# Layer 1's gate weights in two loads instead of four, and pair 0's scores moved ahead of pair 15's maximum product in layer 2

## The chip, the cores and the metric

The kernel runs on one core of a Trainium2 chip. The metric is the time of one execution on the device in microseconds (us); lower is better. Most executions of one kernel agree within 0.3%. The profile of a kernel is one execution taken by the hardware profiler; its span is some 1.4 us shorter than the time of the same execution.

## The reference

The program is a decode step of two identical layers for one token of width 640, in bf16: attention over the last 4096 cached positions, with 32 heads of 192, then a gated MLP of width 1536. Weights are the same in both layers, and so are the caches.

```
x = x + attention(layernorm(x))      # q = x@wq; scores with 4096 keys; softmax; values; @wo
x = x + mlp(layernorm(x))            # (sigmoid(x@w_gate) * (x@w_up)) @ w_down
# and both once more
```

There is one token, so every weight and every cached value is used for one matrix-vector product. The work is reading: 218.7 MB.

## The kernel before

Heads are taken in 16 pairs. A pair has an "a" part (query weights and keys) and a "b" part (values and output weights), 3.6 MB each, in one of seven slots of on-chip memory. MLP weights pass through a smaller region of cells; one cell holds one of the 12 blocks of 128 MLP columns. Layer 2 begins with pairs 14, 15, 0 and 1, most of which are still in memory from layer 1.

All loads stand in one list, `seq`, and are issued in that order from one queue, by SyncE (SP). A load waits until its destination has been read for the last time. So a late product on TensorE (PE) makes the next load late. That matters only if the queue has nothing else left to do by then.

The gate weights (`wg`) and what reuses their cells (cut):

```python
    MW = {"wg0": (0, 0, 3), "wg1": (3, 3, 6), "wg2": (6, 6, 9), "wg3": (9, 9, 12), "u0": (12, 0, 2), "u1": (14, 2, 7),
          "d0": (0, 0, 3), "d1": (3, 3, 6), "u2": (6, 7, 10), "u3": (9, 10, 12), "d2": (11, 6, 9), "d3": (14, 9, 12)}
    #     name: (first cell, first block, end block)
    MAFTER = {"d0": ("wg0",), "d1": ("wg1",), "u2": ("wg2",), "u3": ("wg3",), "d2": ("wg3", "u0"), "d3": ("u1",)}
    ...
            c, f0, f1 = MW[k]
            src = {"w": wg_d, "u": wu_d, "d": wd_d}[k[0]]
            pg.dma(q_dma(mreg(c * FW, (f1 - f0) * FW), src[:, f0 * FW:f1 * FW]), k, wr=rc[c:c + f1 - f0])
```

The first down load `d0` goes into the cells of `wg0`, the third up load `u2` into those of `wg2`. The product is in four parts of three blocks, in the same order.

The start of layer 2's attention (cut). `QK` is the 24 score matmuls of a pair, `soft` takes the maximum on VectorE (DVE) and spreads it over the partitions by the "maximum product" on PE, and `expo` is the exponent on ScalarE (ACT):

```python
            soft(0, scale_pm)                    # pair 14
            expo()
            ET(0)
            Q(0, 0)
            soft(1, hook=lambda: Q(2, None))     # pair 15: max, then the hook, then the maximum product
            for i in (2, 0, 1):
                ...                              # three copies on DVE
            expo(1)                              # pair 15
            QK(0, 0)                             # pair 0's scores; frees slot 4
            soft(0, mid=lambda: PVmm(14, 0))     # pair 0's maximum
```

## Time and profile before

| | |
|---|---|
| time, median of 3 runs | 514.11 us (513.99 to 514.98) |
| span of the profiled run | 512.7 us |
| bytes read, mean rate | 218.7 MB, 427 GB/s |
| busy: 16 DMA engines / PE / DVE / ACT | 99% / 51% / 20% / 17% |

From the profile page of the kernel before: span, busy time of the engines, busy tenths of the DMA engines in 40 slices, packets, the queue that carries the loads (packets, MB, share of 16 engines' span), and the chain of work that ended last by engine.

```profile
span 512.7 us, 8580 instructions
PE 260.9 (51%) x3716; PEld 136.9 (27%) x3716; DVE 100.4 (20%) x379; ACT 84.8 (17%) x171; POOL 4.2 (1%) x31
DMA  9999999999999999999999999999999999999996
DMA packets 9820, 218.71 MB, mean 427 GB/s; under 512 B 1224, under 2 KB 1608, under 8 KB 4808
q1 hardware_dynamic: 9656, 218.37, 99.2%
DMA 63%; PE 23%; DVE 7%; ACT 3%; issue 2%; SPq 2%; DVEq 0%; POOL 0%; ACTq 0%; POOLq 0%
```

The queue table decides: the 16 DMA engines are busy from end to end. The last line alone could mislead. The chain of waits runs through PE for 23% of the span, because a load's issue waits for a product; but while it waits, the queue is still working on older loads.

The useful number is therefore the **backlog**: the landing of the load before, less the issue of this one. It is how long the queue still has to work when a load is added. A load is split over 16 engines, which signal one by one; "landing" here is the last of the 16. From the trace of the kernel before:

| load (bytes per row) | issued | landed | backlog at issue |
|---|---|---|---|
| last gate load (3840) | 261.41 | 277.48 | 14.9 |
| second up load, u1 (6400) | 264.00 | 280.18 | 14.3 |
| first down load, d0 (3840) | 275.25 | 281.34 | 4.9 |
| third up load, u2 (3840) | 276.97 | 283.71 | 5.5 |
| refill of pair 0's slot (28416) | 304.09 | 319.75 | 7.3 |
| first load of the late loop (56832) | 363.72 | 387.39 | 6.9 |

After the first loads it is never below 4.5 us.

The stretch where the gates are used, from the timeline of the kernel before (start us, length us, engine, line, operation, output and inputs, count, and in brackets the idle time before it and what ended that). The gate product is four times 15 matmuls, the first two merged:

```profile
274.69 1.11 PE L675 MATMUL scores<-sh,big 128*128 128x1 bf16 x30 [0.35 <-DVE sc L371]
275.25 0.90 SPq L214 DMA_DIRECT2D big<-in_wd_dram  x2
276.38 0.56 PE L675 MATMUL scores<-sh,big 128*128 128x1 bf16 x15 [0.58 <-DMA big<-in_wg_dram]
276.97 1.48 SPq L214 DMA_DIRECT2D big<-in_wu_dram  x2
277.53 0.56 PE L675 MATMUL scores<-sh,big 128*128 128x1 bf16 x15 [0.59 <-DMA big<-in_wg_dram]
```

The first two parts wait for the layernorm, not for weights. The third and fourth wait for their loads, and each releases a load 0.6 us later.

The start of layer 2, from the same view: pair 15's own scores, pair 15's maximum (DVE L439), its maximum product (PE L445), pair 0's scores (PE L429), the three copies (DVE L170), the refill that the scores release, and pair 0's maximum.

```profile
293.51 1.48 PE L429 MATMUL o<-big,qs 128*32 128x512 bf16 x24
298.80 1.22 DVE L439 TENSOR_REDUCE sc<-o 128x1 f32<-128x1024 f32 x1
300.57 0.79 PE L445 MATMUL bank<-diag,sc 128*128 128x128 f32 x2 [1.02 <-ACT diag L442]
301.29 2.75 PE L429 MATMUL scores<-big,qs 128*32 128x512 bf16 x24
301.83 1.94 DVE L170 TENSOR_SCALAR big<-bank 128x507 uint32<-128x507 uint32 x3
304.09 0.33 SPq L214 DMA_DIRECT2D big<-in_uc_dram  x1
304.10 1.23 DVE L439 TENSOR_REDUCE sc<-scores 128x1 f32<-128x1024 f32 x1 [0.32 <-PE scores L429]
```

PE is idle for 1.02 us before the maximum product, although pair 0's scores could run there.

### The profile page before, as it was taken

How to read it: one execution, taken by the hardware profiler on the slowest of the kernel's cores; microseconds unless marked ns; L12 is line 12 of the kernel's file. 1: busy time of each engine (PE TensorE's matmuls, PEld its weight loads, DVE VectorE, ACT ScalarE, POOL GpSimd, SP SyncE). 2: the span in 40 equal slices, each digit the busy share in tenths (PEclk: the TensorE clock that was granted, in tenths of full speed). 3: DMA queues.
4: the chain of work that ended last, by engine and by line, in shares of the span. 5: the costliest groups of instructions: out<-in, count | busy, mean ns of one | idle time of the engine just before them, and what ended most of it. 6: DMA issues, size and time to landing. Idle time of an engine off the chain costs nothing.

```text
span 512.7 us, 8580 instructions
## 1 busy us (share of the span) xinstructions
PE 260.9 (51%) x3716; PEld 136.9 (27%) x3716; DVE 100.4 (20%) x379; ACT 84.8 (17%) x171; POOL 4.2 (1%) x31
## 2 busy tenths in 40 slices
PE   0452456344634454326566767873625244634665
PEld 0221222122312221112234434432312122312334
DVE  0221221111210221112121243321202111210311
ACT  1110111011101111011121033130301011101220
POOL 0010000000000000000000000000000000000000
PEclk9995555566556566675575578665857556556675
DMA  9999999999999999999999999999999999999996
GB/s 426 430 423 426 427 430 428 426 435 448 439 430 426 440 430 430 426 435 457 399 422 416 418 440 436 435 430 427 443 443 443 430 426 426 440 431 417 431 427 275
DMA packets 9820, 218.71 MB, mean 427 GB/s; under 512 B 1224, under 2 KB 1608, under 8 KB 4808
## 3 DMA queue, kind: packets, MB, share of 16 engines
q1 hardware_dynamic: 9656, 218.37, 99.2%
q8 instruction: 13, 0.21, 0.1%
q10 hardware_dynamic: 144, 0.06, 0.0%
q14 instruction: 7, 0.06, 0.0%
HBM read 218.43 MB, written 0.00 MB: 426 GB/s over the span
## 4 chain that ended last, share of the span: by engine, by line
DMA 63%; PE 23%; DVE 7%; ACT 3%; issue 2%; SPq 2%; DVEq 0%; POOL 0%; ACTq 0%; POOLq 0%
DMA big<-in_uc_dram 54%; PE scores L429 9%; PE o L488 7%; DMA big<-in_wd_dram 6%; DMA big<-in_wu_dram 3%; DVE sc L439 3%; PE bank L445 2%; PE bank L411 2%; SPq L214 2%; ACT e_sb L453 2%; PE bank L523 1%; PE bank L459 1%; ACT diag L442 1%; DVE sc L471 1%; PE o L469 1%
## 5 line engine op out<-in xcount | busy, mean ns | idle before, releaser
L429 PE MATMUL scores<-big,qs 128*32 128x512 bf16 x744 | 83.6, 619 | 10.3 <-DVE qs L417 9.6
L411 PE MATMUL bank<-sh,big 128*128 128x1 bf16 x465 | 17.2, 166 | 133.3 <-DMA big<-in_uc_dram 130.9
L488 PE MATMUL o<-big,et_sb 128*2 128x384 bf16 x1024 | 76.1, 465 | 6.1 <-DMA big<-in_uc_dram 3.6
L442 ACT ACTIVATE diag<-cst,sc 128x128 f32<-128x128 bf16 x32 | 12.8, 401 | 310.2 <-DVE sc L439 299.3
L439 DVE TENSOR_REDUCE sc<-scores 128x1 f32<-128x1024 f32 x31 | 37.9, 1224 | 79.1 <-PE scores L429 79.1
L411 PEld LDWEIGHTS bank<-sh,big 128*128 128x128 bf16 x465 | 14.7, 104 | 136.5 <-DMA big<-in_uc_dram 113.2
L445 PE MATMUL bank<-diag,sc 128*128 128x128 f32 x64 | 21.8, 436 | 46.7 <-ACT diag L442 46.7
L453 ACT ACTIVATE e_sb<-scores,sc 128x1024 bf16<-128x1024 f32 x31 | 37.3, 1204 | 39.7 <-DVE sc L448 37.4
L417 DVE TENSOR_TENSOR qs<-bank,cst 128x96 bf16<-128x96 f32 x30 | 7.7, 258 | 163.6 <-PE bank L411 163.6
L488 PEld LDWEIGHTS o<-big,et_sb 128*2 128x2 bf16 x1024 | 27.8, 106 | 41.7 <-issue 28.6
L429 PEld LDWEIGHTS scores<-big,qs 128*32 128x32 bf16 x744 | 24.2, 134 | 45.0 <-issue 33.2
L495 ACT CAST o_sb<-o 128x384 bf16<-128x384 f32 x64 | 29.6, 474 | 21.4 <-PE o L488 21.3
L445 PEld LDWEIGHTS bank<-diag,sc 128*128 128x128 f32 x64 | 13.6, 265 | 71.5 <-ACT diag L442 70.5
L523 PE MATMUL bank<-sh,big 128*128 128x1 bf16 x480 | 17.3, 165 | 15.5 <-DVE sh L512 14.9
L463 DVE CAST et_sb<-bank 128x64 bf16<-128x64 f32 x32 | 7.2, 225 | 69.8 <-PE bank L459 69.8
L523 PEld LDWEIGHTS bank<-sh,big 128*128 128x128 bf16 x480 | 14.6, 99 | 18.0 <-DVE sh L512 12.4
L446 DVE TENSOR_REDUCE sc<-bank 128x2 f32<-128x128 f32 x32 | 9.3, 292 | 40.1 <-PE bank L445 40.1
L459 PE MATMUL bank<-cst,e_sb 128*128 128x8 bf16 x256 | 11.7, 169 | 7.8 <-ACT e_sb L453 7.6
L459 PEld LDWEIGHTS bank<-cst,e_sb 128*128 128x128 bf16 x256 | 9.0, 101 | 23.9 <-issue 17.4
L469 PE MATMUL o<-sc 128*128 128x2 f32 x62 | 13.8, 292 | 0.6 <-ACT o_sb L495 0.6
L469 PEld LDWEIGHTS o<-sc 128*128 128x128 f32 x62 | 11.9, 239 | 1.9 <-ACT o_sb L495 1.3
L471 DVE RECIPROCAL sc<-o 64x1 f32<-64x1 f32 x62 | 10.2, 164 | 10.0 <-PE o L469 8.2
(78 smaller groups left out, 105.9 us busy)
## 6 DMA issues: line engine op xcount, KB each, us to landing
big<-in_uc_dram SPq DMA_DIRECT2D x20, 7104.0 KB, 22.7
big<-in_uc_dram SPq DMA_DIRECT2D x11, 3552.0 KB, 21.4
big<-in_uc_dram SPq DMA_DIRECT2D x2, 3072.0 KB, 18.8
big<-in_uc_dram SPq DMA_DIRECT2D x7, 480.0 KB, 6.5
big<-in_uc_dram SPq DMA_DIRECT2D x1, 2784.0 KB, 12.3
big<-in_uc_dram SPq DMA_DIRECT2D x1, 2304.0 KB, 10.0
big<-in_uc_dram SPq DMA_DIRECT2D x1, 2048.0 KB, 11.7
big<-in_wg_dram SPq DMA_DIRECT2D x4, 480.0 KB, 15.1
```

The source lines that it names most:

```text
L411: ins = t.matmul(qe[:, i:i + 1], lhsT=w[:, c * 2 * DH + c0:c * 2 * DH + c0 + P], rhs=xq[:, c:c + 1], start=(c == 0), stop=(c == DC - 1))
L429: ins = t.matmul(sc_x[1 + b][32 * j:32 * j + 32, :], lhsT=qs[:, y, k, :], rhs=slot(sa, WQE + k * W + (4 * b + j) * 512, 512), start=(k == ...
L439: pg.op("dve", lambda v: v.reduce_max(out=mx, in_=sc_x[0][:], axis=AX.X), wr=[res("mx")], ex=sc_x[3:5])
L442: pg.op("act", lambda a: a.mul(out=diag[:], in_=ident, mul=mx), rd=[res("cst"), res("mx")], wr=[res("diag")])
L445: pg.op("pe", lambda t: t.matmul(dmx[:, 0:P], lhsT=ones_f, rhs=diag[:], start=True, stop=True), rd=[res("diag"), res("ones")], ex=[rb[2]])
L453: pg.op("act", lambda a: a.activation(out=e_sb[:], in_=sc_x[0][:], func=ACT.Exp, bias=nbias, scale=srs_c, accum_out=rowsum), rd=[res("nbia ...
L459: ins = t.matmul(qe[:, 0:2 * NB].rearrange("p (r x) -> p r x", r=2)[:, :, 4 * b:4 * b + 4], lhsT=e_sb[:, b * P:(b + 1) * P], rhs=sel, star ...
L469: pg.op("pe", lambda t: t.matmul(sm, lhsT=ones_f, rhs=rs2[z], start=True, stop=True), rd=[res(f"rs2{z}"), res("ones")], wr=[res("rsum")], ...
L471: rb[bk].last["dve"] = pg.op("dve", lambda v, h=h: v.reciprocal(out=Rn[z][64 * h:64 * h + 64], in_=sm[64 * h:64 * h + 64, h:h + 1]), rd=[r ...
L488: ins = t.matmul(o8[h][32 * j:32 * j + 2, 0:2 * DH].rearrange("p (a d) -> p a d", a=2), lhsT=et_sb[:, z, h * NB + 2 * u:h * NB + 2 * u + 2 ...
L495: pg.op("act", lambda a, h=h: a.copy(out=o8_sb[:, :, h * DH:(h + 1) * DH], in_=o8[h][:, 0:2 * DH].rearrange("p (a d) -> p a d", a=2)), wr= ...
L523: ins = t.matmul(yT[:, j:j + 1], lhsT=wo[:, c * D + j * P:c * D + (j + 1) * P], rhs=oTb[z][:, c:c + 1], start=False, stop=(c == 2), skip_g ...
```

## The change

The intent: larger and fewer transfers for the gate weights, and PE's gap in layer 2 filled, with a slot freed earlier.

```diff
+    MD = {"wg0": (0, 0, 6), "wg2": (6, 6, 12), **{k: v for k, v in MW.items() if k[0] != "w"}}
...
-    ... [(k,) for k in (*MW, "v1", ...)] ...
+    ... [(k,) for k in (*MD, "v1", ...)] ...
...
-            c, f0, f1 = MW[k]
+            c, f0, f1 = MD[k]
...
-            soft(1, hook=lambda: Q(2, None))
+            soft(1, hook=lambda: (Q(2, None), QK(0, 0)))
...
             expo(1)
-            QK(0, 0)
             soft(0, mid=lambda: PVmm(14, 0))
```

The product is still in four parts, but the first two now wait for one load and the last two for the other. One line was added, so line numbers after it are one higher.

More of the change, by code (lines that the diff above doesn't have):

```diff
@@ L229, in decode_kernel @@
     seq = [("a", 0, 0)] + [("c", 0, p) for p in range(1, 15)] + [("a", 0, 15), ("b", 0, 14)] + last_values(0, 15)
-    seq += [("wol", 14), ("wol", 15)] + [(k,) for k in (*MW, "v1", "wq2", "v0", "v2", "v3", "v4", "wq3", "wom")] + [("a0", 1), ("a0", 2), ("a", 1, 3), ("b", 1, 2)]
+    seq += [("wol", 14), ("wol", 15)] + [(k,) for k in (*MD, "v1", "wq2", "v0", "v2", "v3", "v4", "wq3", "wom")] + [("a0", 1), ("a0", 2), ("a", 1, 3), ("b", 1, 2)]
     seq += [("b", 1, 3), ("a", 1, 4), ("b", 1, 4), ("a", 1, 5), ("a", 1, 6), ("b", 1, 5)]
@@ L299, in try_load @@
             pg.dma(q_dma(slot(s, o, WOE), b_in(it[1], o, o + WOE)), f"wol{it[1]}", wr=[res(f"wol{it[1]}")], extra=ev_done["b1" if it[1] == 15 else "b14"])
-        elif k in MW:
+        elif k in MD:
             if any("done_" + n not in ev_done for n in MAFTER.get(k, ())):
                 return False
-            c, f0, f1 = MW[k]
+            c, f0, f1 = MD[k]
             src = {"w": wg_d, "u": wu_d, "d": wd_d}[k[0]]
```

## The prediction

> **What bounds the kernel.** The 16 DMA engines. The queue table puts queue 1 at 99.2% of 16 engines' span; 218.7 MB in 512.7 us is 427 GB/s. PE is busy 51%, DVE 20%, ACT 17%. Pairing each issue in the trace with its landing gives the backlog, the time the queue still had to work when the next load was issued: never below 4.5 us after the start. Tightest are layer 1's MLP (issues at 275 to 290 us: 4.5 to 5.7 us) and the steady loops (5.2 to 7). The first load's first packet began 1.0 us after its issue, the last store's 1.3 us after, so 4.5 us is enough. A compute change counts only if it lets the backlog run out, or changes what the engines carry.
>
> **Gate weights in two loads.** Four 480 KB loads (rows of 3840 B) become two of 960 KB (rows of 7680 B). In the trace a 3840 B packet takes 149 ns and a 7680 B one 291 ns: 7 ns saved for each of 256 packets, over 16 engines 0.11 us; two loads' completion writes (9 ns each on every engine) add 0.02 us. Two issues of 0.43 us go from SP, but SP was 13 to 15 us ahead there, so that is worth nothing. The direction agrees with the Trainium skill, "Perfetto Trace Analysis", section "DMA Optimizations" (larger transfers use bandwidth better), but here it is 2% on under 1% of the bytes.
>
> The cost: the first six blocks land together near 275.1 us, so the gate product starts there, not at 274.66; the second six near 277.4, where its first half had been there at 276.33. Loads that reuse the cells go later: first down load 275.25 to about 275.8, third up load 276.97 to about 278.05. Backlog falls by about 1 us at most, to some 4.3 us, still enough: no time lost.
>
> **Pair 0's scores earlier.** PE runs the 24 score matmuls (2.75 us) at about 299.5 us, in the 1.0 us gap before pair 15's maximum product (300.57), not after it. Pair 0's slot is released about 1.7 us earlier: its refill is issued at about 302.4 instead of 304.09. But the maximum product moves to about 302.3, pair 15's exponent from 301.93 to about 303.6, and three copies on DVE that stand before pair 0's maximum from 301.83 to about 303.5; pair 0's maximum goes from 304.10 to about 305.4. The compute chain gets 1 to 1.4 us longer until about 345 us. Backlog at those issues is 7 to 18 us, so neither gain nor loss reaches the end; from 363 us the loop is paced by landings again.
>
> **Sum.** About -0.13 us on the DMA stream, 0 from the rest: 514.0 us, range 513.3 to 514.7, wide because the runs before span 513.99 to 514.98. Faster by over 2%: 0.005; within 2%: 0.99; slower: 0.005.
>
> **What would show it.** Right: queue 1 still about 99% and 427 GB/s; 256 packets of 7680 B for 512 of 3840 B; last gate load landing within 0.2 us of 277.4; maximum product about 1.7 us later and pair 0's maximum later, while loads from 350 us land within 0.3 us of before. Wrong: a gap in DMA near 278 to 284 us, or landings from 290 us on shifted by over 0.5 us.
>
> **What would make it wrong.** If a load under traffic needs much more than 1.3 us from issue to data, the smaller backlog in the MLP starves the engines and costs up to 1 us; or the packet rate drifts between builds by more than the effect, a quarter of a thousandth.

## The result, and the profile after

| | median | runs |
|---|---|---|
| before | 514.05 us | 6, 513.75 to 514.98 |
| changed | 514.02 us | 6, 513.67 to 514.52 |
| ratio | 0.9998 | 95% interval 0.9985 to 1.001 |

A ratio is the mean time of one kernel's fast runs over that of the other's fast runs of the same rounds, so it is not quite the ratio of the medians. The result is "the same".

The same lines of the page for the changed kernel:

```profile
span 513.1 us, 8577 instructions
PE 265.5 (52%) x3716; PEld 140.1 (27%) x3716; DVE 100.4 (20%) x379; ACT 84.8 (17%) x171; POOL 4.3 (1%) x31
DMA  9999999999999999999999999999999999999996
DMA packets 9532, 218.71 MB, mean 426 GB/s; under 512 B 1192, under 2 KB 1576, under 8 KB 4520
q1 hardware_dynamic: 9368, 218.37, 99.2%
DMA 64%; PE 23%; DVE 7%; ACT 2%; issue 2%; SPq 1%; DVEq 0%; ACTq 0%
```

Bytes are the same, and q1 has 288 packets fewer: 256 of data and 32 that signal the completion of two loads. Its share stays at 99.2%.

The loads, from the list of DMA issues on the pages (count, KB each, median us from issue to landing), before and then after:

```profile
big<-in_wg_dram SPq DMA_DIRECT2D x4, 480.0 KB, 15.1
```

```profile
big<-in_wg_dram SPq DMA_DIRECT2D x2, 960.0 KB, 16.1
```

The gate stretch of the changed kernel, from its timeline:

```profile
274.98 0.96 PE L675 MATMUL scores<-sh,big 128*128 128x1 bf16 x30 [0.88 <-DMA big<-in_wg_dram]
275.56 0.80 SPq L215 DMA_DIRECT2D big<-in_wd_dram  x2
277.27 0.96 PE L675 MATMUL scores<-sh,big 128*128 128x1 bf16 x30 [1.34 <-DMA big<-in_wg_dram]
277.87 0.80 SPq L215 DMA_DIRECT2D big<-in_wu_dram  x2
```

Both halves of the product now wait for their load. The first down load goes out 0.3 us later than before, and the third up load 0.9 us later. Their backlogs are 4.3 and 4.6 us.

The start of layer 2 of the changed kernel, from the same view:

```profile
293.72 2.75 PE L430 MATMUL o<-big,qs 128*32 128x512 bf16 x24
300.59 1.22 DVE L440 TENSOR_REDUCE sc<-o 128x1 f32<-128x1024 f32 x1
301.29 2.75 PE L430 MATMUL scores<-big,qs 128*32 128x512 bf16 x24
303.97 0.49 PE L446 MATMUL bank<-diag,sc 128*128 128x128 f32 x2
304.09 0.33 SPq L215 DMA_DIRECT2D big<-in_uc_dram  x1
304.94 1.94 DVE L170 TENSOR_SCALAR big<-bank 128x507 uint32<-128x507 uint32 x3
306.80 1.21 DVE L440 TENSOR_REDUCE sc<-scores 128x1 f32<-128x1024 f32 x1
```

Read naively, the change gained nothing at the refill (304.09 in both) and cost 2.7 us at pair 0's maximum. But the first line shows that the two executions differ before the moved instructions are reached: pair 15's own 24 matmuls took 1.48 us in one and 2.75 us in the other. The granted clock of PE differs: it went to full at 292.9 us in the kernel before, ahead of this group, and only at 297.2 us, after it, in the changed kernel. The change is not needed for that, as a second execution of the changed kernel will show. The Trainium skill, "TensorE: Matmul & The Clock Gate", section "Part 1: The HAM clock gate (the 'warmup' mystery)", says that the clock is decided in a free-running window of about 3.4 us, so that the same kernel can meet it in different phases. The traces agree: in their clock records the clock is half or full, each stretch but the last is a whole multiple of 3.41 us long, and the identical group takes 1.48 or 2.75 us, a factor of 1.86, in runs of identical code (the first experiment).

A last difference: the slowest of the 16 engines fell back by 1.5 us in one load, issued at 285 us (landing 292.93 us, before 291.39). The prediction had named landings from 290 us on that shift by over 0.5 us as a sign that it was wrong. The experiments had to tell whether that is the change's doing.

### The profile page after: what moved, and what is told of

The parts are those of the page before. It is cut to its first block, busy times and chain, and to the rows that moved or that the text cites. A ratio compares the mean times of both kernels' runs of the same rounds, so it can differ in the third digit from the quotient of the medians.

```text
span 513.1 us, 8577 instructions
## 1 busy us (share of the span) xinstructions
PE 265.5 (52%) x3716; PEld 140.1 (27%) x3716; DVE 100.4 (20%) x379; ACT 84.8 (17%) x171; POOL 4.3 (1%) x31
## 3 DMA queue, kind: packets, MB, share of 16 engines
q1 hardware_dynamic: 9368, 218.37, 99.2%
## 4 chain that ended last, share of the span: by engine, by line
DMA 64%; PE 23%; DVE 7%; ACT 2%; issue 2%; SPq 1%; DVEq 0%; ACTq 0%
DMA big<-in_uc_dram 54%; PE scores L430 9%; PE o L489 6%; DMA big<-in_wd_dram 6%; DMA big<-in_wu_dram 4%; DVE sc L440 3%; PE bank L446 2%; PE bank L412 2%; PE bank L524 1%; SPq L215 1%; ACT diag L443 1%; ACT e_sb L454 1%; PE bank L460 1%; DVE sc L472 1%; DVE qs L418 1%
## 5 line engine op out<-in xcount | busy, mean ns | idle before, releaser
L489 PE MATMUL o<-big,et_sb 128*2 128x384 bf16 x1024 | 77.8, 471 | 6.2 <-DMA big<-in_uc_dram 3.9
```

The lines of the kernel that those rows point to most:

```text
L489: ins = t.matmul(o8[h][32 * j:32 * j + 2, 0:2 * DH].rearrange("p (a d) -> p a d", a=2), lhsT=et_sb[:, z, h * NB + 2 * u:h * NB + 2 * u + 2 ...
```

## The experiments

The theory, T1: the DMA stream sets the time; both parts of the change are off the path, because the backlog is never used up. The rivals: R1, both parts matter and cancel; R2, the thinner backlog after the gates starves an engine, and the slip at 285 us is its trace; R3, the compute chain at the start of layer 2 sets the pace there.

Twelve kernels ran, in three calls of four. All gave correct results. Each is an edit of the changed kernel, except `hold_g2`, which is an edit of the kernel before. In the tables, "d" is the median less that of the kernel before in the same call.

### First call: once more, each part alone, and the loads made smaller

**again** is the changed kernel, unedited.

> The changed kernel itself, once more. T1 (the DMA stream sets the time, both parts are off the path): 514.0 us, within 0.1% of before. In the profile of the changed kernel the last of 16 engines fell 1.5 us behind in the load of 6400 B rows issued at 285 us (landing 292.93 against 291.39), and a 16 KB instruction fetch ran at 289.4. If this slip belongs to the change (R2: the thinner backlog starves an engine) it comes again at the same load with 1.5 us; if it is chance which engine the fetch hits (T1), the landing of this load is nearer to 291.3 in about half of the executions, or slips elsewhere. Two fewer DMA issues, and the first engine's landing of the third up load again near 281.9 (281.7 before).

**gates_only** puts the scores back:

```diff
-            soft(1, hook=lambda: (Q(2, None), QK(0, 0)))
+            soft(1, hook=lambda: Q(2, None))
             ...
             expo(1)
+            QK(0, 0)
```

> Only the gate loads are joined; the scores stand where they stood. T1: 0.02% faster than before at most (0.13 us), not to be told from 1.000; last gate load lands 0.1 to 0.3 us earlier, third up load issued about 0.9 us later. R1 (the two parts each matter and cancel): slower than before by 0.5 us or more (0.1%), because the gate product starts later. The scores chain as before: maximum product of pair 15 near 300.6 us, pair 0's maximum near 304.1.

**scores_only** loads the gates in four again:

```diff
-    MD = {"wg0": (0, 0, 6), "wg2": (6, 6, 12), **{k: v for k, v in MW.items() if k[0] != "w"}}
+    MD = {**{k: v for k, v in MW.items()}}
```

> Only the scores stand earlier; the gates come in four loads. T1: 1.000 of before within 0.05%; pair 15's maximum product 2 to 3 us later than before, the loads of layer 2's start issued 1 to 4 us later, landings from 350 us on within 0.5 us of before. R1: faster than before by 0.5 us or more (the other half of the cancellation).

**gates12** loads them in twelve:

```diff
-    MD = {"wg0": (0, 0, 6), "wg2": (6, 6, 12), **{...}}
+    MD = {**{f"wgs{i}": (i, i, i + 1) for i in range(12)}, **{...}}
```

> The gate weights in twelve loads of one block (rows of 1280 B) in place of two. By the packet times of the trace (55 ns for 1280 B, 291 for 7680 B): 1536 x 55 / 16 = 5.28 us against 256 x 291 / 16 = 4.66 us on each engine, and ten more completion writes of 9 ns: T1 expects 0.7 us more than the changed kernel (514.7 us, ratio 1.0011 to before), and 0.6 us more than before, all of it by the last gate load's landing. If the queue takes only some nine loads at a time (the issue of the tenth was held up before), the backlog in this stage drops to about 4 us and up to 1 us more may come on top. A theory in which the joined loads gain through fewer issues (ten more x 0.43 us = 4.3 us of SP) expects about 4 us more.

| run | median us | d | ratio (95%) | gate stream, mean of 16 engines |
|---|---|---|---|---|
| before | 514.01 | | | 4.67 us |
| again | 514.08 | +0.07 | 1.0002 (0.9989 to 1.0015) | 4.61 us |
| gates_only | 514.36 | +0.35 | 1.0006 (0.9994 to 1.0018) | 4.69 us |
| scores_only | 514.08 | +0.07 | 1.0003 (0.9990 to 1.0016) | 4.67 us |
| gates12 | 514.45 | +0.44 | 1.0014 (1.0001 to 1.0027) | 5.01 us |

The last column is from the traces: the landing of the last gate load, less that of the load ahead of the gates, each averaged over the 16 engines. The profiled run of the changed kernel has 4.62 us.

R1 finds no support. Neither part moves the time by an amount that can be told from zero, and no part alone is faster. But the intervals reach from -0.5 to +0.9 us. So R1 at its smallest, 0.5 us for each part in opposite directions, is not excluded by the times, and the sign of each part's own effect stays open.

R2's slip did not return in `again`: the load issued near 285 us landed at 291.09 us, and the last load landed at 510.22 us (before 510.24, changed kernel's first profile 510.63). It did return elsewhere. Against the kernel before, the last engine fell back at this load by 0.5 to 1.6 us in six of the other 13 profiles: the first of the changed kernel, `gates_only`, and four runs described further on (`gates1`, `hold`, `scores4`, `hold_g2`). In the seven others it fell back by under 0.2 us. All six have later issues after the gates, but so have five of the seven, and a link with the change is not excluded by this count. But the backlog at this load is 4.4 to 4.5 us in all 14, so the slip is no sign of a thinner one there, and the kernel before has a slip of its own, 0.6 us, at the load that landed at 304.11 us.

What is seen at both places is an instruction fetch of 16 KB on the DMA engines, at the first of them in all 14 profiles (at 289.1 us before, at 289.4 us in the first profile of the changed kernel; at 301.1 us before for the other slip). The record shows that such a fetch costs time, because one of them falls at different places in different executions. The load of 7104 KB that lands near 113 us takes 16.77 to 16.79 us on the mean of the engines in eleven profiles, and 16.87 us in the three (changed kernel, `gates_only`, `gates1`) in which a fetch runs near 109 us. That is 0.1 us, or some 1.5 us added over the 16 engines. If the engine that is hit is ahead of the others, the last landing shows nothing; if it is the slowest, the landing slips. This last step is inferred: the packets in the trace do not name their engine, and no run tested it.

`gates12` confirms the direction of the packet arithmetic and its rough size: the stream is 0.39 us longer than with two loads, where the packet times had promised 0.7 us. The 0.43 us that each issue takes on SP do not count: ten more of them would have been 4.3 us. SP was held up in issuing the twelve, as the expectation had allowed for, but the backlog at them never fell below 6.4 us.

`again` also answers the naive reading. From its timeline:

```profile
293.23 1.48 PE L430 MATMUL o<-big,qs 128*32 128x512 bf16 x24
298.52 1.22 DVE L440 TENSOR_REDUCE sc<-o 128x1 f32<-128x1024 f32 x1
299.20 2.75 PE L430 MATMUL scores<-big,qs 128*32 128x512 bf16 x24
301.89 0.70 PE L446 MATMUL bank<-diag,sc 128*128 128x128 f32 x2
302.00 0.33 SPq L215 DMA_DIRECT2D big<-in_uc_dram  x1
304.92 1.21 DVE L440 TENSOR_REDUCE sc<-scores 128x1 f32<-128x1024 f32 x1
```

Here pair 15's matmuls took 1.48 us, as in the kernel before. Counted from pair 15's maximum (298.52, before 298.80), the maximum product comes 1.6 us later, the refill 1.8 us earlier and pair 0's maximum 1.1 us later. That is what the prediction said. As a reordering of compute, the move costs more than it gains: it fills a gap of 1.0 us and opens one of 1.92 us before the next value products, which must wait for pair 15's exponent.

### Second call: how much backlog is needed, and how much slack the start of layer 2 has

**gates1**: one load for all gates, so that the first down load can be issued only after it has landed.

```diff
-    MD = {"wg0": (0, 0, 6), "wg2": (6, 6, 12), **{...}}
+    MD = {"wg0": (0, 0, 12), **{...}}
```

> The gate weights in one load of twelve blocks. It lands near 277.2 us; the first down load can be issued only after the first three blocks' product, near 277.9, where the up loads end at 279.9: backlog 2.0 us. In the changed kernel the first of the 16 engines waited 0.4 us at the third up load, 2.5 us after its issue, so about 2.9 us from issue to data under traffic is an estimate from that. With 2.9 us: the stream loses about 0.9 us (514.9 us), visible as the first down load's landing at 281.9 to 282.3 instead of 281.3. With the prediction's 1.3 us: no loss, 514.0 us, landing 281.2.

**hold**: the first down load, and with it the five behind it, waits for the product of the second up load.

```diff
-    MAFTER = {"d0": ("wg0",), ...}
+    MAFTER = {"d0": ("wg0", "u1"), ...}
...
-            pg.dma(..., k, wr=rc[c:c + f1 - f0])
+            pg.dma(..., k, wr=rc[c:c + f1 - f0], extra=[ev_done["done_u1"]] if k == "d0" else ())
```

> The first down load, and so the five loads behind it, are held until the second up load's product is done (near 280.8 us), 0.9 us after the queue's last landing at 279.9: the backlog runs out on purpose. T1 with 2.9 us from issue to data: a gap in DMA of about 3.8 us, all of it in the end time: 517.5 to 518 us. With 1.3 us: 2.2 us, 516.2 us. A theory in which the chain of products, not the loads, sets the pace of this stage expects at most the wait itself, or nothing where the loop later makes it up: under 1 us.

**scores2** and **scores4**: pair 0's score matmuls two and four times over. The first of the three terms overwrites what stood there, so the result is the same.

```diff
-                for k in ks:
+                for k in ks * (2 if (l, p) == (1, 0) else 1):     # 4 in scores4, 8 in scores8
```

> Pair 0's 24 score matmuls in layer 2 run twice (the second writes the same result over the first): 2.75 us more on the compute chain at the start of layer 2. T1: the backlog there is 8 to 15 us, and 5.7 us at the first load of the loop (365 us), so nothing or up to 0.5 us: 514.0 to 514.5 us. A theory in which the chain of pairs 14, 15 and 0 bounds the start of layer 2 (the reason for moving the scores) expects 2.7 us more: 516.8 us.

> The same four times: 8.25 us more on the chain, more than the backlog of 8 us at the load that waits for these scores (slot 4, issued at 304.1) and more than the 5.7 us at 365 us. T1: the queue runs dry; with 2.9 us from issue to data some 3 us are lost at the first place and 1 to 3 us at the second: 517 to 520 us, with a visible gap in DMA near 312 us. The chain theory: 8.2 us more, 522 us. If nothing in this stretch reached the queue: 514 us.

| run | the late load | issued | backlog | median us | d | ratio (95%) |
|---|---|---|---|---|---|---|
| before | | | | 514.04 | | |
| gates1 | d0 | 277.73 | 2.0 us | 516.05 | +2.0 | 1.0042 (1.0025 to 1.0059) |
| hold | d0 | 280.72 | -0.9 us | 517.79 | +3.75 | 1.0075 (1.0058 to 1.0092) |
| scores2 | slot 4 | 306.58 | 4.5 us | 514.46 | +0.4 | 1.0007 (0.9990 to 1.0024) |
| scores4 | slot 4 | 307.79 | 2.9 us | 515.03 | +1.0 | 1.0023 (1.0007 to 1.0040) |

`hold` shows what a lost backlog looks like. From the windows of 2 us of the kernel before (for each engine busy us and count, then granted clock, DMA share and GB/s):

```profile
278.00:280.00 2.00, 0.78 (x16) 0.70 (x13) 0.40 (x2) 0.73 (x3) 0.00 (x0) 0.50 1.03 421
280.00:282.00 2.00, 1.36 (x40) 1.23 (x40) 0.23 (x1) 0.00 (x0) 0.00 (x0) 0.50 0.99 397
282.00:284.00 2.00, 0.82 (x25) 0.73 (x25) 0.00 (x0) 0.00 (x0) 0.00 (x0) 0.50 1.04 422
```

The late issue in `hold`, and the same windows:

```profile
280.72 0.80 SPq L215 DMA_DIRECT2D big<-in_wd_dram  x2
```

```profile
278.00:280.00 2.00, 0.99 (x23) 0.91 (x21) 0.40 (x2) 0.73 (x3) 0.00 (x0) 0.50 0.19 75
280.00:282.00 2.00, 0.69 (x25) 0.60 (x23) 0.23 (x1) 0.00 (x0) 0.00 (x0) 0.50 0.30 29
282.00:284.00 2.00, 0.00 (x0) 0.00 (x0) 0.00 (x0) 0.00 (x0) 0.00 (x0) 0.50 0.75 267
```

The rate falls to 75, 29 and 267 GB/s. The slowest engine had emptied its queue at 279.81 us; the load came at 280.72 us and landed at 284.64 us, where a load of this size takes 1.2 us when the queue is full. So 3.6 us were lost there (284.64 - 279.81 - 1.19), and the execution ended 3.75 us later. Nothing was made up in the remaining 230 us: the mean landing of the 16 engines was 4.0 us later than in the kernel before at this load, and 4.1 us later at the end. Loss and backlog give the lead that a load needs: 3.6 - 0.9 = 2.7 us from its issue until the slowest engine works on it. In `gates1` the same sum is 0.9 + 2.0 = 2.9 us. The prediction had taken 1.3 us, the time from an issue into an idle queue to the first packet, for the last store (1.0 us for the first load). In `hold` the first packet did begin 0.96 us after the issue, but 15 of the packets that followed took 0.3 to 1.0 us too long.

`gates1` lost more than expected, 2.0 us against 0.9. About 0.9 us went at the first down load, as expected. A further 0.7 us went at the third up load, which was issued with 4.6 us of backlog. A lead of 2.9 us does not explain that, and why it happened is not settled. This run had 20 packets in the stretch that took over 0.3 us too long, where the kernel before had none.

`scores2` behaves as T1 said: 2.75 us were added in program order, the refill was issued 2.5 us later than in the kernel before, and the time did not move beyond the noise. R3, with 516.8 us, falls. `scores4` missed its expectation (517 to 520 us). Its 96 matmuls took 6.74 us, not 11, because PE was granted the full clock for most of that run of work:

```profile
301.00 6.74 PE L430 MATMUL scores<-big,qs 128*32 128x512 bf16 x96
```

So the refill was issued only 3.7 us later, with 2.9 us of backlog left, just at the lead that `gates1` and `hold` had shown, and about 1 us was lost in time. At the load itself the slowest engine lost more, 1.9 us by the formula used above (320.96 - 310.69 - 8.42, the last being what this load takes from a full queue), which would make the lead 4.8 us. The mean engine lost 0.8 us there. So the end time followed the mean more closely here.

### Third call: which half, what counts, and past the edge

With both gate loads joined, some profiles showed packets between 277 and 286 us that took over 0.3 us too long (6.2 us of excess in all in the first profile of the changed kernel, 3.6 in `gates_only`, 4.4 in `scores2`, 0.8 in `scores8` below, none in `again` and `scores4`); with four or twelve loads there were none. So the faster engines seem to be at their edge at times. In the first profile of the changed kernel the mean landing went from 0.3 us ahead of the kernel before, at the second up load, to 0.2 us behind it at the third, and did not come back; in `again` it stayed 0.2 to 0.3 us ahead. The next runs asked which load does it, and whether it matters.

**gates_first** and **gates_last** join one half only:

```diff
-    MD = {"wg0": (0, 0, 6), "wg2": (6, 6, 12), **{...}}
+    MD = {"wg0": (0, 0, 6), **{k: v for k, v in MW.items() if k not in ("wg0", "wg1")}}              # gates_first
+    MD = {**{k: MW[k] for k in ("wg0", "wg1")}, "wg2": (6, 6, 12), **{... if k[0] != "w"}}           # gates_last
```

> Only the first six gate blocks are joined; the scores stand earlier. In the profiles so far packets that take over 0.3 us too long between 277 and 286 us appear only with both gate loads joined (6.2 us in all for the changed kernel, 3.6 and 4.4 us in two other runs of it or its part, 0 in two), never with four loads (0 in two) or twelve (0). Theory E (the later issue of the third up load, 277.7 to 277.9 in place of 277.0, lets the fastest engines run out): here it is issued near 277.0 again and there are none; time 514.0 us. If it is the first down load (275.5 in place of 275.2) that starves them: up to 4 us of such packets again, last landing averaged over the engines 509.1 in place of 508.6 to 508.8 us.

> Only the last six gate blocks are joined; the scores stand earlier. Theory E (third up load, issued near 277.7): overlong packets near 280 to 282 us in some executions, at most 0.4 us on the mean over the engines; none near 278 us, where the first down load's packets run. Time within 0.1% of before, 514.0 to 514.4 us. A theory in which a load of 7680 B rows itself is slower would show it in the gate stream: over 4.7 us on the mean from the last output-weight load to the last gate load, where four loads took 4.67 and two 4.61.

**hold_g2** is the kernel before with the first down load held until the third part of the gate product:

```diff
-    MAFTER = {"d0": ("wg0",), ...}
+    MAFTER = {"d0": ("wg0", "wg2"), ...}
...
-            pg.dma(..., k, wr=rc[c:c + f1 - f0])
+            pg.dma(..., k, wr=rc[c:c + f1 - f0], extra=[ev_done["done_wg2"]] if k == "d0" else ())
```

> The kernel before, with the first down load held until the third gate product is done, near 277.0 us: backlog 3.2 us at the slowest engine, 1.9 us on the mean of the 16, 1.2 us at the fastest. Two runs with less backlog gave backlog plus loss, on the mean, as 2.23 us (one load: 1.05 + 1.18) and 2.25 us (held: -2.1 + 4.35). Theory: every engine loses what its own backlog lacks of 2.25 us, here 1.0 us at the fastest, nothing at the slowest, about 0.5 us on the mean: first down load lands at 280.6 on the mean (280.1 before), end about 0.5 to 1 us later: 514.5 to 515.0 us. If only the slowest engine's backlog counted, as the prediction took it: 514.0 us.

**scores8** is `scores4` with eight.

> Pair 0's score matmuls eight times. Four times gave less delay than expected (3.7 us at the load that waits for them, not 8.25), because the longer run of matmuls was granted the full clock. Eight times: about 12.8 us in place of 2.75 if the full clock lasts, the load issued near 314 us where the engines run out at 309.5 us on the mean. Theory: loss = issue + 2.25 us - mean landing of the load before it, some 6.5 us if it is issued at 314, all of it in the end: 520 us (519 to 522). If the compute chain set the time: 524 us or more. If this stretch had slack that the loop gives back later: under 517 us.

| run | the late load | issued | backlog | median us | d | ratio (95%) |
|---|---|---|---|---|---|---|
| before | | | | 514.19 | | |
| gates_first | d0 | 275.40 | 4.4 us | 513.97 | -0.2 | 0.9994 (0.9980 to 1.0007) |
| gates_last | u2 | 277.76 | 4.3 us | 513.90 | -0.3 | 0.9997 (0.9983 to 1.0010) |
| hold_g2 | d0 | 276.54 | 3.2 us | 513.90 | -0.3 | 0.9998 (0.9985 to 1.0012) |
| scores8 | slot 4 | 311.46 | -0.65 us | 519.32 | +5.1 | 1.0101 (1.0074 to 1.0129) |

`hold_g2` does not bear out what I had expected of it, 514.5 to 515.0 us. Averaged over the engines, the down load did start 0.4 us late and stayed so (last landing on the mean 508.99 us, against 508.60 in `again`), and one could see it in the overlong packets (3.0 us of excess). The rate dipped, as this window of `hold_g2` shows beside the 421 GB/s of the kernel before:

```profile
278.00:280.00 2.00, 0.55 (x19) 0.47 (x19) 0.40 (x2) 0.73 (x3) 0.00 (x0) 0.50 0.88 335
```

But the time did not move beyond the noise, and the slowest engine's last landing was 510.13 us, against 510.24 before. The last product waits for all 16 engines, so an engine that is ahead of the slowest could be starved a little for nothing. That would make the slowest engine's backlog, as the prediction counted it, the right one. It is not shown: the interval ends at +0.6 us, so the lower edge of my expectation is still inside it, and `scores4` spoke for the mean.

`gates_first` and `gates_last` have no overlong packets in their one profile each (nor had `again`) and give gate streams of 4.65 us, between four loads (4.67) and two (4.61). So which load starves the fast engines when both halves are joined stays open. Neither is distinguishable from the kernel before in time, and no version here beats both kernels.

`scores8` goes past the edge in layer 2. The windows of the kernel before at 310 us, then of `scores8`:

```profile
308.00:310.00 2.00, 1.36 (x39) 1.03 (x43) 0.58 (x3) 0.51 (x1) 0.00 (x0) 0.99 1.02 440
310.00:312.00 2.00, 2.00 (x36) 0.87 (x28) 0.06 (x1) 1.52 (x4) 0.00 (x0) 0.50 1.02 439
```

```profile
308.00:310.00 2.00, 2.00 (x44) 1.02 (x40) 0.00 (x0) 0.00 (x0) 0.00 (x0) 1.00 0.52 217
310.00:312.00 2.00, 1.83 (x30) 0.78 (x22) 0.13 (x1) 0.00 (x0) 0.00 (x0) 1.00 0.00 0
```

The engines stand still for 2 us. The load landed 4.2 us later than a full queue would have delivered it (323.44 - 310.81 - 8.42), and this execution was 518.3 us, 4.1 us over the median before. Had it been issued at 314 us, as I had assumed, the formula of the expectation would have given 6.5 us; with 311.46 us it gives 3.9 us, and the mean engine lost 3.8 us at this load. The lead at the slowest engine, loss and backlog added, is 3.6 us here (4.21 - 0.65), more than the 2.7 to 2.9 us of the small loads. The other three runs of it lay between 517.6 and 520.8 us; the granted clock, which sets how long the 192 matmuls take, is the likely reason, but only one run has a profile. R3 falls here too: it had expected 524 us or more. The stretch has slack up to the lead that the queue needs, and none beyond.

## Why the prediction was right, point by point

- **The time.** 514.0 us predicted, 514.02 measured. That the two agree to 0.02 us is luck, as the interval is 0.6 us wide to either side; "the same" is what was shown. The forecast of "the same" rested on the DMA engines as the only limit. `hold` and `scores8` show that the end time follows the queue: in `hold` idle time of the slowest engine came out at the end nearly one for one (3.6 us lost, 3.75 us later).
- **The gain in the stream** was mis-sized. The packet times (149 and 291 ns) promised 0.11 us plus 0.02 us of completion writes. The mean gate stream went from 4.67 to 4.62 and 4.61 us, by 0.05 to 0.06 us, and not at all in `gates_only` (4.69). `gates12` shows the same factor: 0.39 us for a computed 0.7. A likely reason is that packets of one engine overlap a little (the DMA share in this stage is above 1.00), so that their durations add up to more than the time they take; no run isolates it. The direction of the skill's advice on larger transfers ("Perfetto Trace Analysis", section "DMA Optimizations") holds, at a size that the time does not show.
- **The later issues** came as predicted, a little smaller: first down load 275.56 (275.8 predicted), third up load 277.87 (278.05), lowest backlog 4.3 us (4.3).
- **"4.5 us is enough"** was right, for a reason that was half wrong. The lead that the small loads of this stage need is 2.7 to 2.9 us at the slowest engine, not 1.3. By that the change left a margin of 1.4 us, not 3.0. `hold_g2`, with 3.2 us, still lost nothing that the times show; `gates1`, with 2.0 us, lost 2 us of time. The margin is an estimate: part of the loss in `gates1` came at 4.6 us of backlog, and whether the slowest or the mean engine counts is open.
- **The reordered scores** did what was said in the execution with the same clock (`again`): product +1.6 us (1.7), refill -1.8 us (-1.7), pair 0's maximum +1.1 us (1.3). In the first profile a lower granted clock had put everything some 1.8 us later before that. There the refills after that of pair 0's slot were late until 365 us (365.18 against 363.72). In `again` the refill at 340 us was already 0.7 us early, so the "about 345 us" of the prediction held. The 0.9 us by which `again` was late at 364 us is not a mark of the move, as `gates_only`, with the scores where they stood, was 1.1 us late there.
- **The signs.** "Loads from 350 us within 0.3 us of before" was 0.2 to 0.4 us in the first profile, and under 0.2 us in `again`. The sign against the prediction, a shift of over 0.5 us from 290 us on, did appear, and was false: the time did not follow, and `again` did not have it. The shift had shrunk to 0.4 us at the end of that profile. The landing of the last of 16 engines in one profile is no measure for effects of a few tenths of a microsecond.

## What to carry to other kernels

When one queue of transfers is full from end to end, cost a change by two things only: what it alters in the bytes and packets that the queue carries, and whether any load is issued with less backlog than the lead the queue needs. Measure that lead by holding one load back on purpose. Look at the slowest engine, since the last product waits for it, and at the mean of the engines too; which of them the end follows is not settled here. A rearrangement of compute inside the slack is free in both directions, so it can neither be praised nor blamed for a difference of 0.1%.

## What the Trainium skill lacked or had wrong

- "DMA: Bandwidth & Descriptors", section "Latency and other measured facts", gives about 0.6 us to the first byte for loads issued from SP. The traces agree if one counts from the end of the issuing instruction: the first packet into an idle queue came 0.62 us after it for the first load, 0.64 us in `hold` and 0.63 us in `scores8` (1.0 us after the start of the instruction). What the page lacks is how far ahead a queue must be fed to stay full. Here backlog and loss at the slowest of the 16 engines added up to 2.7 and 2.9 us for small loads, and to 3.6 and 4.8 us for loads of 3552 KB; 3.2 us of backlog cost nothing that the times show, 2.9 us about 1 us and 2.0 us about 2 us.
- "Runtime: NRT & Kernel Launch", section "Instruction fetch mechanics", calls the cost of crossing a 16 KiB boundary of the instruction stream "mostly hidden". That is said of the engine that executes. But the profile of the kernel before has 13 fetches of 16 KB among the packets of its DMA engines, of 0.88 to 0.96 us each, and a load into which one falls takes 0.1 us longer on the mean of the 16 engines (16.87 against 16.77 to 16.79 us), some 1.5 us added over them. The page does not give this cost for a kernel whose DMA engines are full.
- No page says by how much packet durations in a trace overstate what packets cost in a full stream: 0.7 us computed from them was 0.39 us in the stream.
